# Rows in runs of 16 and gated values written in token order

## Chip, cores, metric

One core of a Trainium2 chip. The metric is the device time of one execution in microseconds. Every run is compared with runs of the kernel before on the same chip in the same rounds; ratios are the mean time of one kernel's fast runs over the mean of the other's fast runs of those rounds, so they are not quite the ratio of the medians quoted. "Busy" time counts overlapping instructions of an engine once.

## The reference

```python
def phi(x):                                  # x: [8, 8, 576, 64], feature map with 128 projections
    proj = np.einsum('bhsd,df->bhsf', x, w_phi)
    proj = proj - np.max(np.abs(proj), axis=-1, keepdims=True)
    return np.concatenate([np.exp(proj), np.exp(-proj)], axis=-1)
q_p, k_p = phi(q), phi(k)
kv = einsum('bhsf,bhsd->bhfd', k_p, v);  z = k_p.sum(2)
x = einsum('bhsf,bhfd->bhsd', q_p, kv) / (einsum('bhsf,bhf->bhs', q_p, z)[..., None] + 1e-06)
# heads side by side -> x: [8, 576, 512]; then a gated linear unit with a causal convolution of 5 taps
gate = 1 / (1 + exp(-causal_conv(x, conv_w)))
out  = (gate * (x @ w_val)) @ w_out
```

## The kernel before

A task graph is built in Python. The literal strings `ORDER`, `FLEX` (which engine takes a task that two could do), `BANKS` and `WARM` fix the order of instructions on every engine; no scheduler runs at build time. Tokens of a head come in pairs; the 288 pairs of a head are held in an order (k, y, x) with 2, 18 and 8 values, and pair (k, y, x) is token pair (8k + x) * 18 + y. "Unit" u holds four of the 18 y's (the last one two).

```python
    def qexp(self, t, b, u, s):              # feature exponentials of the queries, on ACT
        ...
        if u < 4:
            o = self.QTIL[b % 2][:, s, :, :, :].rearrange("p a h (k r) -> p a (h k) r", k=2)[:, :, :, u * 32:(u + 1) * 32]
            self.nc.scalar.activation(o, i, AF.Exp, scale=1.0 - 2.0 * s)
        else:
            for a in range(2): ...           # the tail: two instructions
    # numerator chunk c = rows 128 of half k: needs the units 0..3, so the graph lets it wait for every exponential
    allq = [G("qexp", b, u, s) for u in range(NU) for s in range(2)] + [G("kv", b, i) for i in range(2)]
    ...
    def gv(self, t, b, j):                   # (1 + tanh) * val, on DVE: one instruction, two PSUM banks
            nc.vector.scalar_tensor_tensor(
                out=self.GV[b % 3][:, j, :, :], in0=self.TH[j][:, :, :], scalar=1.0,
                in1=self.two(t.grp, R), op0=ALU.add, op1=ALU.mult)
    ...
    def odma(self, t, b, c, i0, i1):         # output rows, scattered
            d = self.out_d[b].rearrange("(k x y a) o -> a k y x o", k=2, x=8, a=2)[c % 2, c // 2, 0:16, :, :]
            nc.sync.dma_start(d, O[:, :])
```

On POOL, `vs` scales V by the key exponentials (VT) and `c_gt` builds the convolution taps (SC, GF, GQ). On SP, in one queue, stand the loads of V, the transposing transfers of keys and queries, and the outputs; in the trace of the kernel before they are issued in their order in it (a load of V at 36.55 us, the transpose behind it at 37.11).

## Time and profile before

| what | before |
|---|---|
| time, median of the first three runs | 230.46 us |
| span of the profiled execution | 228.5 us |
| PE, DVE, ACT, POOL busy | 205.4, 176.3, 180.7, 102.8 us |
| gating on DVE | 32 instructions, 23.7 us |

### The profile page before, as it was taken

The numbers are of one execution on the slowest core, as the hardware profiler recorded it, in microseconds if no ns is written. First come the engines' busy times: TensorE is split into PE (matmuls) and PEld (weight loads), VectorE is DVE, ScalarE is ACT, GpSimd is POOL, SyncE is SP. The second block draws the span as 40 slices with busy tenths as digits, with TensorE's granted clock in tenths as the row PEclk, the third lists the DMA queues.
The fourth block names the chain that finished last, engine by engine and source line by source line (L and its number), as shares of the span: only waits on it lengthen the run. The fifth ranks groups of instructions, "written<-read, shape, count | busy, mean of one in ns | idle before, by whom it ended". The sixth has DMA issues, their size and how long they took to land.

```text
span 228.5 us, 9138 instructions
## 1 busy us (share of the span) xinstructions
PE 205.4 (90%) x4001; PEld 142.6 (62%) x4027; DVE 176.3 (77%) x264; ACT 180.7 (79%) x266; POOL 102.8 (45%) x158
## 2 busy tenths in 40 slices
PE   7668887798988999989999999999999999999990
PEld 3345555666675676757667677676765866766640
DVE  2686785998879895989699979788798899483361
ACT  2995999889899988988899999979988999913220
POOL 2718594496029608930099009910119639100020
PEclk9997999999999999999999999999999999999998
DMA  6999943999699939995899995969964206156156
GB/s 202 315 265 286 209 78 103 224 196 183 113 187 244 191 93 179 293 199 61 176 225 182 279 219 141 190 127 228 291 222 138 53 3 142 49 77 204 46 180 188
DMA packets 49282, 39.87 MB, mean 174 GB/s; under 512 B 33690, under 2 KB 38554, under 8 KB 49178
## 3 DMA queue, kind: packets, MB, share of 16 engines
q1 hardware_dynamic: 43136, 29.76, 52.6%
q0 software_dynamic: 5760, 9.31, 24.1%
q8 instruction: 31, 0.51, 0.9%
q10 hardware_dynamic: 346, 0.22, 0.3%
q14 instruction: 9, 0.07, 0.1%
HBM read 30.49 MB, written 9.44 MB: 175 GB/s over the span
## 4 chain that ended last, share of the span: by engine, by line
PE 53%; DVE 17%; DMA 4%; issue 3%; ACT 3%; POOL 2%; DVEq 0%; ACTq 0%
PE PS L751 13%; PE PS L775 10%; PE PS L732 7%; PE PS L598 5%; PE PS L555 5%; DVE XN L691 4%; DMA kT<-KQN 4%; DVE MQP L562 3%; PE PS L670 3%; DVE MK L562 3%; PE PS L739 3%; DVE GV L757 2%; PE PS L642 2%; PE PS L699 2%; PE PS L649 2%
## 5 line engine op out<-in xcount | busy, mean ns | idle before, releaser
L588 POOL TENSOR_TENSOR VT<-VN,EK 128x1152 bf16<-128x1152 f32 x31 | 65.8, 2123 | 60.2 <-ACT EK L581 50.8
L572 ACT ACTIVATE KTIL<-PS 128x1024 bf16<-128x1024 f32 (+1 forms) x80 | 72.5, 951 | 6.3 <-PE PS L555 3.1
L657 ACT ACTIVATE QTIL<-PS 128x1024 bf16<-128x1024 f32 x64 | 62.6, 1036 | 4.6 <-PE PS L649 4.0
L562 DVE TENSOR_REDUCE MQP<-PS 128x8 f32<-128x1024 f32 (+1 forms) x40 | 44.1, 1112 | 6.7 <-PE PS L555 5.6
L562 DVE TENSOR_REDUCE MK<-PS 128x8 f32<-128x1024 f32 (+1 forms) x40 | 44.0, 1110 | 2.5 <-PE PS L555 1.4
L751 PE MATMUL PS<-XT,WV 64*128 64x288 bf16 x512 | 35.5, 283 | 0.4 <-DVE XN L691 0.2
L757 DVE SCALAR_TENSOR_TENSOR GV<-TH,PS 128x576 bf16<-128x576 bf16 x32 | 23.7, 751 | 15.5 <-PE PS L751 10.9
L775 PE MATMUL PS<-WOUT,GV 128*128 128x512 bf16 x109 | 29.6, 380 | 1.5 <-issue 0.6
L743 ACT ACTIVATE TH<-PS 128x576 bf16<-128x576 f32 x32 | 20.1, 655 | 13.0 <-PE PS L739 12.9
L751 PEld LDWEIGHTS <-WV 64*128 64x128 bf16 x512 | 24.6, 94 | 8.3 <-issue 2.6
L598 PE MATMUL PS<-VT,KTIL 64*128 64x65 bf16 x1152 | 24.1, 191 | 1.4 <-POOL VT L589 0.5
L598 PEld LDWEIGHTS <-KTIL 64*128 64x128 bf16 x1152 | 21.3, 95 | 4.2 <-issue 1.3
L691 DVE TENSOR_TENSOR XN<-PS,RCP 128x512 bf16<-128x512 f32 x32 | 22.1, 691 | 1.1
L670 PE MATMUL PS<-KV,QTIL 128*128 128x65 bf16 x512 | 20.1, 193 | 1.7 <-DVE GV L757 0.5
L670 PEld LDWEIGHTS <-QTIL 128*128 128x128 bf16 x512 | 18.2, 97 | 5.0 <-issue 2.7
L612 ACT ACTIVATE OUTS<-PS 128x512 f32<-128x512 f32 x22 | 13.3, 606 | 9.8 <-PE PS L775 9.1
L732 PE MATMUL PS<-XT,GF 128*64 128x288 bf16 x256 | 20.6, 290 | 0.4 <-DVE MQP L562 0.2
L720 POOL COPY XT<-XT 128x224 bf16<-128x224 bf16 x8 | 3.0, 374 | 34.4 <-DVE XT L716 22.3
L775 PEld LDWEIGHTS <-GV 128*128 128x128 bf16 x128 | 11.0, 97 | 11.6 <-issue 1.1
L555 PE MATMUL PS<-W,kT 64*128 64x128 bf16 x288 | 14.9, 219 | 2.7 <-ACT kT L522 1.4
L555 PE MATMUL PS<-W,qT 64*128 64x128 bf16 x288 | 15.1, 220 | 1.7 <-ACT KTIL L572 0.9
L642 PE MATMUL PS<-qT,W 64*128 64x512 bf16 (+1 forms) x80 | 15.0, 359 | 0.9 <-ACT QTIL L657 0.5
(74 smaller groups left out, 257.6 us busy)
## 6 DMA issues: line engine op xcount, KB each, us to landing
VN<-in_v_dram SPq DMA_DIRECT2D x8, 1152.0 KB, 6.9
out_dram<-OUTS SPq DMA_DIRECT2D x32, 256.0 KB, 3.4
KQN<-in_q_dram POOLq DMA_DIRECT2D x6, 576.0 KB, 6.5
KQN<-in_k_dram POOLq DMA_DIRECT2D x6, 576.0 KB, 8.3
KTIL<-in_k_dram SPq DMA_DIRECT2D x4, 288.0 KB, 4.2
KTIL<-in_q_dram SPq DMA_DIRECT2D x4, 256.0 KB, 4.4
out_dram<-OUTS SPq DMA_DIRECT2D x14, 64.0 KB, 3.2
QTIL<-in_q_dram POOLq DMA_DIRECT2D x1, 576.0 KB, 10.4
```

Of the source, the lines that this page charges most:

```text
L555: nc.tensor.matmul(self.PS[:, t.grp.banks[par], i * P:(i + 1) * P], X[rows, (c0 + i) * P:(c0 + i + 1) * P], self.W2[rows, :], start=True, ...
L562: self.nc.vector.tensor_reduce(o, self.two(t.grp, n * P).rearrange("p a (c f) -> p a c f", f=F), AX.X, ALU.max, apply_absolute_value=True)
L572: self.nc.scalar.activation(self.KTIL[b % 2][:, s, c0:c0 + n, :, :].rearrange("p c a f -> p a c f"), self.two(t.grp, n * P).rearrange("p a ...
L588: eng.tensor_tensor(self.VT[g][:, s, :, 0:D], self.VN[b % 2][:, NC * g:NC * g + NC, :], e.to_broadcast([P, NC, D]), ALU.mult)
L598: nc.tensor.matmul(self.PS[:, t.grp.banks[ab], (s * 2 + x) * E1:(s * 2 + x + 1) * E1], self.KTIL[b % 2][rows, s, J // 2, J % 2, :], self.V ...
L657: self.nc.scalar.activation(o, i, AF.Exp, scale=1.0 - 2.0 * s)
L670: nc.tensor.matmul(self.PS[:, t.grp.banks[h // 4], (h % 4) * E1:(h % 4 + 1) * E1], Q[:, s, c % 2, h, (c // 2) * P:(c // 2 + 1) * P], self. ...
L691: nc.vector.tensor_tensor(o.rearrange("p (g h) d -> p g h d", g=ng), n[:, :, :, 0:D], rc.unsqueeze(3).to_broadcast([P, ng, 4, D]), ALU.mult)
L732: self.nc.tensor.matmul(self.PS[h2 * D:(h2 + 1) * D, t.grp.banks[par], 0:R], self.GF[:, h, i, :], X[:, h, :, HALO - 8 * s:HALO - 8 * s + X ...
L751: nc.tensor.matmul(self.PS[:, t.grp.banks[par], 0:R], self.WV2[rows, h, j * P:(j + 1) * P], X[rows, h, :, HALO:XW], start=(h == 0), stop=( ...
L757: nc.vector.scalar_tensor_tensor(out=self.GV[b % 3][:, j, :, :], in0=self.TH[j][:, :, :], scalar=1.0, in1=self.two(t.grp, R), op0=ALU.add, ...
L775: nc.tensor.matmul(self.PS[:, t.grp.banks[0], :], lhsT, self.WOUT[:, j, :], start=(j == 0), stop=(j == 3))
```

## The change

The pairs are held as (y, x) with 18 and 16 values. A chunk of 128 rows is then 8 y's, so it needs two units instead of four; the convolution's halo is one copy; a tail exponential is one instruction. The gated values are written in token order, so each output transfer is a plain stripe of rows.

```diff
-    allq = [G("qexp", b, u, s) for u in range(NU) for s in range(2)] + ...
+    allq = [G("qexp", b, u, s) for u in ((0, 1), (0, 1), (2, 3), (2, 3), (4,))[c] for s in range(2)] + ...
 def gv(self, t, b, j):
-            nc.vector.scalar_tensor_tensor(
-                out=self.GV[b % 3][:, j, :, :], in0=self.TH[j][:, :, :], scalar=1.0,
-                in1=self.two(t.grp, R), op0=ALU.add, op1=ALU.mult)
+            for a in range(2):
+                nc.vector.scalar_tensor_tensor(
+                    out=self.GV[b % 3][:, j, a, :].rearrange("p (x y) -> p y x", x=16),
+                    in0=self.TH[j][:, a, :].rearrange("p (y x) -> p y x", x=16), scalar=1.0,
+                    in1=self.PS[:, t.grp.banks[a], 0:R].rearrange("p (y x) -> p y x", x=16), op0=ALU.add, op1=ALU.mult)
 def odma(...):
-            d = self.out_d[b].rearrange("(k x y a) o -> a k y x o", k=2, x=8, a=2)[c % 2, c // 2, 0:16, :, :]
+            d = self.out_d[b].rearrange("(r a) o -> a r o", a=2)[c % 2, i * P:(i + 1) * P, :]
 # cut: gvc (four copies -> one), halo (two -> one), qexp's tail (two -> one), views of XT and of the query projection,
 # and all of ORDER, FLEX, BANKS, WARM, NW (14 -> 11), which are new throughout
```

## The prediction

> **What bounds the kernel now.** I read the page first, then the busy time of each engine in five stretches, then the chain of waits, and last the timelines of POOL and SP in the head. The page gives TensorE as the fullest engine:
>
> ```profile
> PE 205.4 (90%) x4001; PEld 142.6 (62%) x4027; DVE 176.3 (77%) x264; ACT 180.7 (79%) x266; POOL 102.8 (45%) x158
> ...
> PE   7668887798988999989999999999999999999990
> ```
>
> The second line is PE in 40 slices of 5.7 us: loosely packed for ten slices, nearly full afterwards. The stretches (columns PE, PEld, DVE, ACT, POOL busy, then clock, DMA share, GB/s) put numbers on it:
>
> ```profile
> 0.00:30.00 30.00, 22.29 (x244) 13.51 (x247) 19.60 (x25) 21.91 (x33) 16.16 (x34) 0.94 1.00 253
> 30.00:60.00 30.00, 25.05 (x628) 18.22 (x630) 24.29 (x34) 27.46 (x40) 18.35 (x21) 1.00 0.84 157
> 60.00:200.00 140.00, 135.15 (x2859) 96.83 (x2870) 118.44 (x182) 126.00 (x186) 66.19 (x94) 1.00 0.77 169
> 200.00:223.20 23.20, 22.89 (x288) 14.01 (x286) 13.23 (x24) 5.37 (x9) 2.14 (x10) 1.00 0.52 129
> ```
>
> PE idles 12.7 us in the first 60 us, 4.9 us in the next 140 (3.5%), 0.3 us up to its end at 223.2; a fixed tail of 5.3 us (last eviction, its output transfer) follows. Of the busy time, 10.4 us are the warm-up matmuls on a tile of ones (L481), all in the first 60 us. So the 228.5 us are 195.0 of real matmul work, 10.4 of warm-up, 17.8 idle, 5.3 tail. Only two things can shorten it: a shorter head (23.1 us of idle and warm-up in it) or fewer gaps later (5.2 us). ACT, at 27.46 of 30 us, is the fullest engine between 30 and 60.
>
> In the head the chain of waits begins with a transfer, not with an engine:
>
> ```profile
> 37.11 8.90 DMA kT<-KQN
> ...
> 46.06 0.62 PE PS L555 x16
> ```
>
> It is the transpose of the keys of batch 2, issued at 37.11. SP and POOL show why not earlier:
>
> ```profile
> 7.02 29.90 SPq L509 DMA_DIRECT2D VN<-in_v_dram  x3
> 37.11 5.51 SPq L543 DMA_TRANSPOSE kT<-KQN  x1
> ...
> SPq L509 <- POOL VT L589: 18.9, 1, 18.9
> ```
>
> ```profile
> 25.54 1.49 POOL L472 COPY SC<-cwP 64x8 f32<-64x8 f32 x10 [2.19 <-DVE cwP L464]
> 27.11 4.10 POOL L475 TENSOR_TENSOR GF<-SC,ID 128x512 bf16<-128x512 f32 x4
> 31.17 1.06 POOL L477 TENSOR_TENSOR GQ<-SC,ID 128x512 bf16<-128x512 f32 x1
> 32.19 2.12 POOL L588 TENSOR_TENSOR VT<-VN,EK 128x1152 bf16<-128x1152 f32 x1
> 34.25 0.26 POOL L589 CAST VT<-EK 128x18 bf16<-128x18 f32 x1
> 34.40 2.12 POOL L588 TENSOR_TENSOR VT<-VN,EK 128x1152 bf16<-128x1152 f32 x1
> 36.47 0.26 POOL L589 CAST VT<-EK 128x18 bf16<-128x18 f32 x1
> ```
>
> SP's queue is in order, and the third load of V stands in front of the transpose. It overwrites the V of batch 0, so it waits until POOL has scaled that V, at 36.73. POOL is late because it first builds the convolution taps (25.5 to 32.2). The DMA share in 32 to 36 us is 0.06 and 0.00: the transfer could have run.
>
> [...] the reduction takes 1219 ns for 1024 columns and 687 for 512, so 1.04 ns a column and 154 ns fixed. [...] The changed gating writes bf16 at a step of 18 elements, 36 bytes[...]; no DVE instruction of this trace writes so, and the price is open. [...]
>
> **The change part by part.** Rows within a head are ordered with 16 slow positions instead of 2 by 8.
>
> *PE.* The same matmuls and columns. Patterns change (288 contiguous columns instead of 2 by 144, runs of 16 instead of 8 in the query projection), but a projection with 16-byte runs takes 380 ns for 512 columns and the contiguous output matmul also 380, so I count no gain. Warm-up matmuls go from 35 to 30: 5 x 0.3 = 1.5 us less, in the head.
>
> *DVE, gating.* 32 instructions of 751 ns (600 for 576 columns, 151 fixed) become 64 of 300 + 151 = 451: 32 x (902 - 751) = +4.8 us, if the step costs nothing. Work that the new assignment moves: four fp32 copies of keys and queries come over (+4 x 0.68), one small copy (+0.3), three KV casts leave (-3 x 0.70), two output evictions come (+2 x 0.68), one scaling of V leaves (-3.4). Sum +3.7, so about 180 busy.
>
> *ACT.* The tail exponentials: 32 of 401 ns become 16 of about 609 (a 128x512 exponential of the keys). By busy time, which counts overlap once, 10.3 becomes 9.4: -0.9. Moves: -4 x 0.61, -0.4, +3 x 0.63, -2 x 0.61. Sum about -3.0, nearly all in the first 30 us.
>
> *POOL.* Halo 374 + 252 ns and four tail copies of 241 become one of about 390 and one of about 400 (0.83 ns a column plus 188, from 64 and 224 columns). By busy time 11.3 becomes about 6.3: -5.0; one V scaling comes, +2.4. No bound here.
>
> *Dependences.* A numerator chunk waits for four exponentials rather than ten, and a query exponential waits only for the two earlier chunks that read its half. That lets PE fill gaps. In the head of before, though, the first numerator waited 0.46 us for KV, not for an exponential, so the new KV time decides.
>
> *The head, by the new order.* POOL now scales all of V of batch 0 first, and builds the taps after. The second half needs its exponential on ACT, which stands behind the first and about 7 query exponentials: 6 x 0.95 + 0.55 = 6.3 us. The first can come when the query bias is there. DVE has before it 12.2 us of copies, maxima and reductions from 5.8, so it is there about 19 to 20 (21.5 before), and the first exponential at about 21.7, the second at 28. Two scalings, 4.6 us, end at about 32.8 instead of 36.73. So the transpose goes out about 3.9 us earlier, if the loads of queries and keys it reads have landed, which the falling DMA share at 30 to 32 us suggests. ACT, which sets the pace there, has 3.0 us less to do: both point to 3 to 4 us.
>
> PE does not get all of it back, because some of the work that comes earlier only displaces idle in other places: I count 3.0 us. The finer waits may close some of the 4.9 us of gaps between 60 and 200, and the extra 4.8 us of DVE opens others; DVE goes from 118 of 140 to about 121, still under PE. I count -0.3. Span 228.5 - 3.3 = 225.2; the time is 1.8 us above the span in the profiled execution (230.27 against 228.5), so 227.0 us.
>
> **The rivals.** (1) Nothing moves: PE's work is the same, and the gain in latency is hidden behind a PE that is 97% full. For it: the stretch from 60 on. Against: the 23 us lost in the head. Time 229.5 to 230.5. (2) The stepped write doubles the column time of the gating: +32 x 600 ns = 19 us of DVE on top, some 199 in all, which would put DVE at 96% in the middle; gating then ends later, and the output matmuls wait. Time 231 to 236. [...] (3) The head shrinks by the whole 6 us or more, because numerators, gates and values of batch 0 also start earlier, and the finer waits remove half of the gaps: 222 to 224. (4) The transpose is early but the key load behind it lands late (it is issued after the first V scaling, which itself comes 4 us later): the gain shrinks to 1 us, 229.
>
> **Range and chances.** I take 227.0, range 223.8 to 230.6. Faster by over 2% means below 225.85: 0.35, rival 3 and the upper half of the main line. Within 2%: 0.60. Slower: 0.05, rival 2.
>
> **What would show it.** The transpose of kT issued at 33 to 34 instead of 37.1, and the first keys of batch 2 on PE at 42 to 43 instead of 46; idle plus warm-up of PE in the first 60 us at about 20 instead of 23; gap time from 60 to the end of PE near 5; PE's end near 220; gating instructions of 450 ns with DVE at 180; outputs still 3.4 us to landing. A gating of over 700 ns, or the transpose again at 37, would break my reasons; a drop of PE's real busy time below 193 would mean that the patterns do matter for matmuls.

## More of the kernel before

PE is the fullest engine and is nearly full after 60 us; the prediction shows the lines. Two groups that it only cites are given here from the page: the gating (busy time, then mean ns of one, then DVE's idle time before it), and the output transfers (KB each, us from issue to landing).

```profile
L757 DVE SCALAR_TENSOR_TENSOR GV<-TH,PS 128x576 bf16<-128x576 bf16 x32 | 23.7, 751 | 15.5 <-PE PS L751 10.9
...
out_dram<-OUTS SPq DMA_DIRECT2D x32, 256.0 KB, 3.4
```

## The result, and the profile after

The changed kernel takes 292.29 us (median of four runs; one of them was slow) against 230.65: the ratio of the fast runs is 1.264, interval 1.254 to 1.275. The prediction was 227.0 with a range up to 230.6.

From the page of the changed kernel, in the order of the lines shown of before: busy times, PE's forty slices and the clock granted to it, the chain that ended last, and the gating.

```profile
PE 225.8 (78%) x4022; PEld 152.0 (53%) x4022; DVE 230.9 (80%) x298; ACT 180.0 (62%) x246; POOL 100.0 (35%) x128
...
PE   7788977868788689786957689975986898968664
...
PEclk9999999999999999999998979997597999995978
...
DVE 44%; PE 38%; issue 7%; ACT 5%; DMA 4%; DVEq 0%; ACTq 0%
...
L754 DVE SCALAR_TENSOR_TENSOR GV<-TH,PS 128x288 bf16<-128x288 bf16 x64 | 83.0, 1546 | 8.1 <-PE PS L747 7.0
```

ACT and POOL are as long as foreseen. DVE has grown by 54.6 us, and the gating alone by 59.3: one instruction of 288 columns takes 1546 ns, twice what 576 columns took. DVE leads the chain (44%, PE 38%), in which PE had 53% before. The pieces of the chain around 90 us show it (start, length, what), and a line of PE's waits (us in all, times, longest):

```profile
88.11 1.13 PE PS L747 x16
89.24 2.64 DVE GV L754 x2
91.88 0.27 DVE MK L560
92.15 2.56 DVE GV L754 x2
...
PE PS L747 <- DVE GV L754: 6.1, 8, 1.0
```

A value matmul ends, its gating pair takes 2.6 us, and a maximum queued behind it waits in DVE's order. PE waits with it: among its 17 longest groups of waits, those put down to the gating sum to 22.6 us; before, they were 0.9 us. The stretch from 60 to 200 us (PE, PEld, DVE, ACT, POOL busy, clock, DMA share, GB/s):

```profile
60.00:200.00 140.00, 110.25 (x2190) 77.86 (x2184) 122.54 (x161) 93.20 (x127) 44.79 (x52) 0.97 0.71 152
```

Between 60 and 200 us PE is busy 110.3 us where it was 135.2. The matmul instructions are the same; fewer of them are done by then.

In the head the transpose did go out earlier. The chain and POOL's timeline:

```profile
34.50 11.22 DMA kT<-KQN
...
45.77 0.42 PE PS L553 x8
```

```profile
31.80 2.12 POOL L586 TENSOR_TENSOR VT<-VN,EK 128x1152 bf16<-128x1152 f32 x1
33.86 0.26 POOL L587 CAST VT<-EK 128x18 bf16<-128x18 f32 x1
34.00 1.50 POOL L470 COPY SC<-cwP 64x8 f32<-64x8 f32 x10
```

V of batch 0 is scaled by 34.1 us and the taps come after it. The transpose leaves 2.6 us earlier than before (34.50 against 37.11), but takes 11.22 us instead of 8.90, so PE gets the keys at 45.77 instead of 46.06.

### The profile page after: what moved, and what is told of

It reads as the page before. It is cut to its first block, busy times and chain, and to the rows that moved or that the text cites. A ratio compares the mean times of both kernels' runs of the same rounds, so it can differ in the third digit from the quotient of the medians.

```text
span 288.3 us, 9117 instructions
## 1 busy us (share of the span) xinstructions
PE 225.8 (78%) x4022; PEld 152.0 (53%) x4022; DVE 230.9 (80%) x298; ACT 180.0 (62%) x246; POOL 100.0 (35%) x128
## 3 DMA queue, kind: packets, MB, share of 16 engines
q1 hardware_dynamic: 43136, 29.76, 42.0%
## 4 chain that ended last, share of the span: by engine, by line
DVE 44%; PE 38%; issue 7%; ACT 5%; DMA 4%; DVEq 0%; ACTq 0%
DVE GV L754 27%; PE PS L770 9%; DVE MK L560 6%; DVE MQP L560 5%; PE PS L747 5%; PE PS L728 4%; DMA kT<-KQN 4%; PE PS L553 4%; PE PS L596 4%; ACT KTIL L570 3%; PE PS L667 3%; DVE XN L688 2%; PE PS L640 2%; PE PS L735 2%; PE PS L479 2%
## 5 line engine op out<-in xcount | busy, mean ns | idle before, releaser
L586 POOL TENSOR_TENSOR VT<-VN,EK 128x1152 bf16<-128x1152 f32 x32 | 68.1, 2127 | 70.5 <-ACT EK L579 55.8
L754 DVE SCALAR_TENSOR_TENSOR GV<-TH,PS 128x288 bf16<-128x288 bf16 x64 | 83.0, 1546 | 8.1 <-PE PS L747 7.0
L560 DVE TENSOR_REDUCE MK<-PS 128x8 f32<-128x1024 f32 (+1 forms) x40 | 43.9, 1107 | 4.8 <-ACT KTIL L570 2.2
L747 PE MATMUL PS<-XT,WV 64*128 64x288 bf16 x512 | 40.3, 299 | 7.7 <-DVE GV L754 6.1
L770 PE MATMUL PS<-WOUT,GV 128*128 128x512 bf16 x128 | 35.5, 418 | 7.2 <-DVE OUTS L606 4.4
L739 ACT ACTIVATE TH<-PS 128x576 bf16<-128x576 f32 x32 | 19.9, 652 | 29.9 <-PE PS L735 29.7
L747 PEld LDWEIGHTS <-WV 64*128 64x128 bf16 x512 | 27.5, 99 | 16.8 <-issue 10.6
L760 POOL COPY GVT<-GV 128x256 bf16<-128x256 bf16 x8 | 3.2, 403 | 87.7 <-DVE GV L754 64.7
L610 ACT ACTIVATE OUTS<-PS 128x512 f32<-128x512 f32 x20 | 12.1, 603 | 26.7 <-PE PS L770 24.7
L728 PE MATMUL PS<-XT,GF 128*64 128x288 bf16 x256 | 23.2, 307 | 4.6 <-DVE GV L754 3.1
L770 PEld LDWEIGHTS <-GV 128*128 128x128 bf16 x128 | 12.7, 106 | 22.6 <-issue 13.1
L640 PE MATMUL PS<-qT,W 64*128 64x512 bf16 (+1 forms) x80 | 17.6, 374 | 4.5 <-DVE GV L754 2.2
```

The source lines that it names most:

```text
L560: self.nc.vector.tensor_reduce(o, self.two(t.grp, n * P).rearrange("p a (c f) -> p a c f", f=F), AX.X, ALU.max, apply_absolute_value=True)
L586: eng.tensor_tensor(self.VT[g][:, s, :, 0:D], self.VN[b % 2][:, NC * g:NC * g + NC, :], e.to_broadcast([P, NC, D]), ALU.mult)
L728: self.nc.tensor.matmul(self.PS[h2 * D:(h2 + 1) * D, t.grp.banks[par], 0:R], self.GF[:, h, i, :], X[:, h, HALO - 16 * s:HALO - 16 * s + R] ...
L747: nc.tensor.matmul(self.PS[:, t.grp.banks[par], 0:R], self.WV2[rows, h, j * P:(j + 1) * P], X[rows, h, HALO:XW], start=(h == 0), stop=(h = ...
L754: nc.vector.scalar_tensor_tensor(out=self.GV[b % 3][:, j, a, :].rearrange("p (x y) -> p y x", x=16), in0=self.TH[j][:, a, :].rearrange("p ...
L770: nc.tensor.matmul(self.PS[:, t.grp.banks[0], :], lhsT, self.WOUT[:, j, :], start=(j == 0), stop=(j == 3))
```

## The experiments

Theory A: the step of the written values costs, element by element. Rival B: short rows of a three-dimensional pattern cost. Rival C: contention from what runs beside the gating. Rival D: the new order of instructions is poor. The comparison with the reference can't see a permutation of rows here: permuting the rows of the reference as e2 does changes it by 0.2% in norm. Where a kernel is called right below, it is so by its construction.

### e1: a ruler, with nothing beside it

At the end of the kernel before, after its last work:

```diff
+            for _ in range(4):
+                V.scalar_tensor_tensor(out=step(1), in0=th, scalar=1.0, in1=ps, op0=ALU.add, op1=ALU.mult)
+                ...                       # step(s): 288 bf16 elements, s elements apart; s = 2, 4, 8, 9, 16, 18, 32
+                V.scalar_tensor_tensor(out=<the changed pattern>, ...)          # and steps on the reads; copies; ACT; POOL
```

> The kernel before, unchanged, with a ruler behind its last work: gating instructions of 288 columns with the output written at a step of 1, 2, 4, 8, 9, 16, 18 and 32 bf16 elements, then in the changed kernel's pattern, then with the step on the read side (both operands, PSUM alone, the tanh alone), then copies, ACT and POOL in the same two patterns, four times each, with nothing else running. Theory A (the step of the written bf16 is the cost[...]): step 1 about 450 ns, then rising with the step up to 8 elements (16 bytes) and flat from there near 1300 to 1500; the changed pattern as step 18; a step on the reads near 450 or with a smaller price. Theory B (the short rows of a three-dimensional pattern cost, some 60 ns for each of 18 rows): steps with one dimension stay near 450, the changed pattern 1400 to 1500, and the read-side patterns with the same rows as slow. Theory C (contention: the slow gating in the changed kernel comes from what runs beside it): all near 450 here.

Each line is one kind: minimum, median and maximum of four, in ns. L834 to L837 write at steps of 1, 2, 4 and 8, L840 at 18, L842 in the changed pattern; L843 reads both operands at a step of 16, L844 PSUM alone, L845 the tanh alone; L847 copies to bf16 and L848 to fp32, both in the changed pattern (36 and 72 bytes from one element to the next); L849 and L850 are a tanh on ACT, written contiguously and in the changed pattern.

```profile
L834 DVE SCALAR_TENSOR_TENSOR KTIL<-TH,PS x4: 444/454/455, 222.7 to 279.0; 128x288 bf16<-128x288 bf16 x4
L835 DVE SCALAR_TENSOR_TENSOR KTIL<-TH,PS x4: 475/476/476, 223.2 to 279.5; 128x288 bf16<-128x288 bf16 x4
L836 DVE SCALAR_TENSOR_TENSOR KTIL<-TH,PS x4: 791/793/794, 223.7 to 280.0; 128x288 bf16<-128x288 bf16 x4
L837 DVE SCALAR_TENSOR_TENSOR KTIL<-TH,PS x4: 1426/1428/1428, 224.5 to 280.8; 128x288 bf16<-128x288 bf16 x4
L840 DVE SCALAR_TENSOR_TENSOR KTIL<-TH,PS x4: 1383/1384/1387, 228.8 to 285.1; 128x288 bf16<-128x288 bf16 x4
L842 DVE SCALAR_TENSOR_TENSOR KTIL<-TH,PS x4: 1386/1391/1392, 231.7 to 288.0; 128x288 bf16<-128x288 bf16 x4
L843 DVE SCALAR_TENSOR_TENSOR KTIL<-TH,PS x4: 666/668/670, 233.1 to 289.4; 128x288 bf16<-128x288 bf16 x4
L844 DVE SCALAR_TENSOR_TENSOR KTIL<-TH,PS x4: 453/454/455, 233.8 to 290.1; 128x288 bf16<-128x288 bf16 x4
L845 DVE SCALAR_TENSOR_TENSOR KTIL<-TH,PS x4: 669/670/670, 234.3 to 290.6; 128x288 bf16<-128x288 bf16 x4
L847 DVE CAST KTIL<-PS x4: 1389/1392/1393, 235.5 to 291.8; 128x288 bf16<-128x288 f32 x4
L848 DVE COPY KTIL<-PS x4: 641/641/641, 236.9 to 293.2; 128x288 f32<-128x288 f32 x4
L849 ACT ACTIVATE KTIL<-PS x4: 411/411/411, 237.6 to 293.9; 128x288 bf16<-128x288 f32 x4
L850 ACT ACTIVATE KTIL<-PS x4: 1407/1407/1407, 238.1 to 294.3; 128x288 bf16<-128x288 f32 x4
```

Every bf16 line follows theory A. Written bf16 cost next to nothing up to a step of two (476 against 454 ns); with the fixed 151 ns taken off, they cost twice the column time of 300 ns at four (793), four times at eight (1428), and the same beyond (1356 to 1410 at 9, 16, 18 and 32). What makes the step cost is not shown: in the changed pattern a copy to fp32, 72 bytes from one element to the next, takes 641 ns, and one to bf16, at 36 bytes, 1392. The changed pattern (1391) equals a one-dimensional step of 18 (1384), and reads of PSUM with rows as short but a contiguous write are at 454: B falls. A stepped read of the bf16 operand in SBUF takes 670 ns, (670 - 454) / 288 = 0.75 ns an element. Nothing ran beside it: C falls as the cause (a single instruction takes 1546 ns in the kernel and 1391 alone, so at most a tenth is company). The price is (1391 - 454) / 288 = 3.25 ns an element; over 64 x 288 elements, 60 us. ACT pays the same way (3.46 ns an element), and POOL's copy went from 427 to 1415 ns (3.43).

### e2: the changed kernel without the step

```diff
-                    out=self.GV[b % 3][:, j, a, :].rearrange("p (x y) -> p y x", x=16),
+                    out=self.GV[b % 3][:, j, a, :],
```

> The changed kernel with its order, its two gating instructions and its stripes of output, but the gated values written in the order they are computed, without a step (rows of the output then come out permuted: wrong on purpose). Theory A or B: gating falls to about 450 ns each, DVE busy from 231 to about 180, and the time to 226 to 229 us, because nothing else in the change costs. Theory C or a fourth, D (the new order of instructions is itself poor): the time stays above 245 us although gating is short.

Measured: 235.6 us, ratio 1.022 (1.016 to 1.029).

```profile
L754 DVE SCALAR_TENSOR_TENSOR GV<-TH,PS 128x288 bf16<-128x288 bf16 x64 | 25.9, 449 | 7.9 <-PE PS L747 6.5 <-ACT TH L739 1.0
...
60.00:200.00 140.00, 129.55 (x2649) 92.76 (x2666) 115.98 (x200) 118.29 (x164) 63.85 (x71) 0.99 0.78 166
```

The gating gives back 57.1 us of DVE (83.0 to 25.9), and the mean of the fast runs falls by 55.9 (291.6 to 235.7): nearly one for one. But it lands above the expected 226 to 229. PE has 10.4 us of gaps between 60 and 200, where before had 4.9. So D is not dead: a remainder of about 5 us is left for it, which e7 tests.

### e3: the step on the reads

```diff
-                    out=...rearrange("p (x y) -> p y x", x=16),  in0=/in1=...rearrange("p (y x) -> p y x", x=16)
+                    out=...rearrange("p (x y) -> p x y", x=16),  in0=/in1=...rearrange("p (y x) -> p x y", x=16)
```

> The changed kernel with the step moved from the write to the reads: output of the gating contiguous in token order, tanh and PSUM read at a step of 16 elements; the result stays right. Theory A: gating near 450 to 600 ns, time 226 to 232. Theory B: as slow as the changed kernel, 280 to 295, since the rows are as short (18 elements).

Measured: 244.17 us, ratio 1.057 (1.048 to 1.066), a right result; gating 671 ns, as the ruler's 668. B falls again. It is slower than A expected: 13.7 us more gating than e2 (39.6 against 25.9) cost about 8.6 us.

### e4: no token order, scattered rows, one gating instruction

```diff
+            nc.vector.scalar_tensor_tensor(out=self.GV[b % 3][:, j, :, :], ...)          # as before
+            d = self.out_d[b].rearrange("(x y a) o -> a y x o", x=16, a=2)[c % 2, 8 * i:8 * i + 8, :, :]
+            # and the tail copy on POOL as four transposing copies
```

> The change without its token order, right result: one gating instruction of 576 columns as before, written without a step; output rows go out as 8 by 16 scattered rows, and the tail copy on POOL is back to four transposing copies per batch. DVE 5 us less than in e2, but each output transfer has 8 as its slowest dimension instead of 128[...]. Theories A and B: time 225 to 229[...]. If the output transfers hold up the output buffers, 230 to 235, and the stripes were worth having.

Measured: 248.61 us, ratio 1.076 (1.065 to 1.087). A miss, by 14 us or more: this version does less DVE work than e2 and is much slower. It changed three things at once, so e9 and e10 take it apart.

### e5: the kernel before, with the step alone

```diff
-            nc.vector.scalar_tensor_tensor(out=self.GV[b % 3][:, j, :, :], ...)
+            for a in range(2):  ...                        # the two stepped instructions of the change, nothing else
```

> The kernel before with one thing of the change: its 32 gating instructions split into 64 and written at the step of 18 elements (the values land in the wrong columns: wrong on purpose). If the step carries the loss by itself, whatever the order of the rest, DVE rises from 176 to about 235 us busy and the time to 283 to 297, as in the changed kernel. If the new order of instructions or the finer waits multiply it, it stays below 270.

Measured: 288.85 us, ratio 1.246 (1.236 to 1.256); gating 1531 ns, DVE busy 231.0. The step by itself makes nearly all of the loss, in the old order as well as in the new.

### e6: token order by reading PSUM at a step

In the ruler, DVE's reads of PSUM at a step of 16 fp32 cost nothing (454 ns with the step and without). So tanh and gating both read PSUM so, and everything written is contiguous in token order:

```diff
+        self.nc.scalar.activation(self.TH[j][:, :, :].rearrange("p a (x y) -> p a x y", x=16),
+                                  self.two(t.grp, R).rearrange("p a (y x) -> p a x y", x=16), AF.Tanh)
+            out = GV and in0 = TH contiguous;  in1=self.PS[:, t.grp.banks[a], 0:R].rearrange("p (y x) -> p x y", x=16)
```

The gating stays split into two instructions, one for each bank.

> The changed kernel with token order kept, right result, but made by reads of PSUM at a step of 16 fp32 elements: tanh and the gating read PSUM so, and write contiguously. The ruler gave 454 ns for such a gating. If stepped PSUM reads are free for ACT too (tanh near 650 ns), DVE is at 178 and the time equals e2: 234 to 237 us. If ACT pays for them as DVE paid for the tanh (668 ns), ACT rises by 7 us or more and the time to 237 to 241.

Measured: 233.62 us, ratio 1.012 (1.005 to 1.020). Tanh 654 ns (655 before), gating 449: the step is free on this side for both engines. This is the change as it was meant, with a right result, and it is still not faster than before.

### e7: e6 with the old order

```diff
- ORDER, FLEX, BANKS, WARM, NW of the changed kernel
+ those of the kernel before (task numbers agree again with NW = 14)
```

> e6 with the order, the engine choices, the banks and the warm-up of the kernel before: the new layout alone, without the new order. If the 5 us that e2 is still slower than before come from the new order, 228 to 232 us. If they come from the layout (stripes, split gating, finer waits), 234 to 238, as e6.

Measured: 229.70 us, ratio 0.993 (0.988 to 0.999), beside e6's 1.012 of the same rounds. The two stretches of 60 to 200 us, e6 and then e7:

```profile
60.00:200.00 140.00, 128.13 (x2619) 91.97 (x2633) 115.20 (x198) 116.44 (x161) 62.85 (x70) 0.99 0.76 166
```

```profile
60.00:200.00 140.00, 134.47 (x2822) 95.84 (x2833) 119.23 (x203) 124.81 (x174) 63.33 (x70) 1.00 0.77 169
```

The remainder is D: the new order leaves PE 11.9 us of gaps in that stretch, the old one 5.5. Some matmul records are missing in both traces (4000 of 4022 and 4001 of 4027 are there) and read as gaps; two traces without missing records, of e9 (new order) and e11 (old order), give 8.0 and 3.5 us. The layout itself is worth 0.7%, at the edge of the noise.

### e8: the keys of batch 2 loaded earlier

```diff
  POOL:  load q(2), scale V(0) first part, load k(2), ...   ->   load q(2), load k(2), scale V(0) first part, ...
```

> e6 with one move: the load of the keys of batch 2 is issued on POOL before the first scaling of V instead of after it. If the late load is what made the early transpose land no earlier (45.7 us in the changed kernel, 46.0 before, though issued at 34.5 against 37.1), the transpose lands at 41 to 43 and the time falls by 1 to 3 us below e6. If what it waits for is the DMA engines, shared with the load of V of batch 2, the landing stays at 45 to 46 and the time equals e6.

Measured: 233.01 us, ratio 1.010 (1.003 to 1.016), against e6's 1.012: no difference. The key load is issued at 11.53 instead of 25.46. The transpose goes out at 33.76 and lands after 9.0 us, at 42.8; in e6 it goes out at 34.83 and lands after 9.1 us, at 43.9. So the earlier load does not shorten the transfer. PE begins on these keys at 44.21 (45.27 in e6), 1.4 us after they have landed both times and with no wait for them on record: here, an earlier landing is worth nothing.

### e9 and e10: what made e4 slow

e9 is e2 with one contiguous gating instruction; e10 is e9 with e4's scattered chunk transfers alone.

> e2 with one gating instruction of 576 columns instead of two of 288 (again no step, output rows permuted, wrong on purpose). It takes 752 ns against 2 x 449, so DVE loses 1.9 us by the busy times seen in e4 and e2 (24.0 against 25.9). If the split mattered, the time falls 1 to 2 us below e2, to 233 to 235; otherwise equal to e2, 234 to 237. It must not be near e4 (249), unless the single gating is what made e4 slow.

> e9 with e4's output transfers alone for the 32 chunks (8 by 16 scattered rows, slowest dimension 8), tail stripes and tail copy as in the change (wrong on purpose in the tails). If e4's 13 us over e2 come from output transfers[...], 244 to 250 here[...]. If they come from the four tail copies on POOL, 234 to 237.

Measured: e9 232.79 us, ratio 1.008 (0.999 to 1.017); e10 249.02, ratio 1.073 (1.061 to 1.085; its profile fell in a slow execution, the ratio uses fast ones). In e10 rows of the tails were overwritten or left unwritten. What the split gating of e2 costs is not pinned down: e2's ratio is 1.022 and e9's 1.008, from other rounds on another chip, and their intervals overlap. The form of the output transfers is e4's loss: e9 and e10 ran in the same rounds and differ in it alone. PE's longest waits, e9 and then, for a fast profile, e4 from 60 us on (total us, times, longest):

```profile
PE PS L553 <- issue: 2.7, 1, 2.7
```

```profile
PE PS L553 <- DMA kT<-KQN: 5.2, 2, 3.4
PE PS L553 <- issue: 3.6, 1, 3.6
```

In e4 and e10 (5.9 us) PE waits for the transposed keys, in e9 no such wait is on record; why they are late is not shown. The trace gives no landing times for the scattered transfers, but it counts packets: e10 has 43136 - 42880 = 256 fewer than e9 on the page's hardware queue q1, eight for each of the 32 transfers. What that has to do with the time is not shown either.

### e11 and e12: the head, by one move on POOL

e11 is e7, e12 the kernel before, each with both scalings of the second half of V of batch 0 ahead of the taps:

```diff
  POOL:  VT first half, taps (SC, GF, GQ), VT second half   ->   VT first half, VT second half, taps
```

> e7 (new layout, old order) with one move on POOL, the one that the prediction built on: both scalings of the second half of V of batch 0 before the taps. The theory of the head: the transpose of kT goes out at 31 to 32 instead of 37.5 and lands about 5 us earlier than in e7 (46.5); if PE's head is paced by it, the time falls by 2 to 5 us below e7, to 225 to 228. If ACT and the other engines pace the head anyway, the transpose is early and the time stays at 229 to 230.

> The kernel before with e11's move on POOL alone, nothing of the change. If the gain of e11 is that move (2.5 us against e7) and the new layout adds little (e7 was 0.7% under before), this is at 227.5 to 229.5 us; if the layout is what makes the move pay, it stays at 230 to 231.

Measured: e11 227.23 us, ratio 0.986 (0.981 to 0.992): it beats both kernels. e12 228.68, ratio 0.990 (0.985 to 0.995). SP of e11:

```profile
30.46 0.37 SPq L473 DMA_DIRECT2D VN<-in_v_dram  x1
33.93 3.48 SPq L507 DMA_TRANSPOSE kT<-KQN  x1
```

The load of V goes out at 30.46, 6.5 us earlier than in e7 (36.93), the transpose only at 33.93, 3.6 earlier (37.49). It lands after 6.0 us, at 39.9, and PE uses its keys at 44.53 (46.50 in e7), so PE is not waiting for it. The median is 2.5 us under e7's, at the low end of what was expected, but from other rounds on another chip; by the two ratios it is 0.7%, 1.6 us. The move alone gives 1.0% (e12); the layout's share on top is within the noise. In both, PE's idle and warm-up in the first 60 us sum to 19.9 us, where before had 23.1.

## Why the prediction was wrong, point by point

**The step that failed: the term for the gating, "64 of 300 + 151 = 451 ... +4.8 us, if the step costs nothing".** One instruction took 1546 ns, and the gating's busy time grew by 59.3 us. The cost was named (rival 2), but as a doubling worth 19 us, and held at 0.05. Both were estimates: no DVE instruction of the trace wrote at such a step, and the prediction itself calls the price open. The ruler shows it: 3.25 ns for each stepped element on top of a column time of 1.04 ns, so a write like this takes four times the column time, not twice.

**What followed from it.** I took PE to stay the bound, at "DVE goes from 118 of 140 to about 121". DVE was at 122.5 of 140, but with PE at 110 and most of the work later: the stretch was simply longer. With 59 us more, DVE's total passed PE's, and nearly each us of it showed in the time (57.1 against 55.9 in e2). The gaps also go with a lower granted clock on PE, 0.944 on average against 0.989; what that adds was not isolated.

**The head.** Earlier issue: right (34.50 for a predicted 33 to 34). Keys on PE at 42 to 43: wrong, 45.77. In the changed kernel the transfer took 11.2 us to land, not 8.9, and PE waited for it. That isn't the new order by itself: e6, with the same order, landed it in 9.1 us, at 43.9, and PE still used the keys only at 45.27. So this transfer isn't all that paces PE there; what else does is open. Idle and warm-up of PE in the first 60 us, by the sum 60 - (46.6 - 10.4), is 23.8 us, not 20. (A small slip: 28 and the 4.6 us of two scalings make 32.6, not 32.8.)

Rival 4 gave the outcome in the head, but its reason, the late key load, fell with e8. What does go with the length of the transfer is the load of V in front of it: 0.6 us behind that load's issue it took 8.9 to 11.2 us (before, changed, e6, e7, e8), 3.5 and 5.2 us behind it 6.0 and 5.0 us (e11, e12). The reason is not shown: no run changed this alone. In the old order the same move on POOL was worth 1.6 to 2.5 us (e11) and 1.7 to 2.3 us (e12), by medians and by ratios: somewhat under my 3.0.

**The gaps.** "-0.3" for the finer waits less DVE's additions: wrong by some 4 us of time (e6 against e7). Without the step, the new order has 8.0 to 11.9 us of gaps from 60 to 200 (e9, e2, e6) instead of 4.9, and the old order with the same layout 3.5 to 5.5 (e11, e7). I judged the order only by its head. Which of its positions costs is open. The largest single wait in e2 is this one, in a query or key projection (the chain, start and length):

```profile
130.07 0.27 PE PS L553 x5
130.34 2.63 issue
```

A transpose of keys was on its way from 128.13, with an issue of 6.93 us. That this is its wait is likely, but the trace names no releaser.

**What held.** PE's real work: in e6, 204.3 less 8.5 of warm-up, 195.8, against 195.0, each with some records missing, and 195.5 in e9 with none missing; patterns cost PE nothing that these traces show. ACT 178.7 in e6 for a predicted 177.7; POOL 100.0 for about 100; halo 389 ns and tail copy 403 for 390 and 400; DVE without the step 177.8 for 180. Output transfers were to stay at 3.4 us to landing; they landed in 2.6 to 3.1 in all versions with stripes and a short gating, 2.7 in e7 with the old order: the stripes are faster, off the critical path.

## What to carry to other kernels

When a reorder has to happen somewhere, put the step on a read of PSUM and keep the writes contiguous: here the stepped bf16 write paid 3.3 to 3.5 ns an element on top, on DVE, ACT and POOL alike, and the stepped read of PSUM nothing, on DVE (454 ns) and ACT (654 for 655). A price that no row of the profile shows is not a price of zero: measure it by itself, or give its rival a weight and a size to match. And judge a new instruction order over the whole kernel, for a gain in its head can be lost in gaps later.
